# Attention and a gated feed-forward on one core: dense rows of seven tokens for the whole first batch, g's product moved, and a schedule planned with newly fitted transfers

## The chip, the cores and the metric

The kernel runs on one core of one Trainium2 chip. The metric is the device time of one execution in microseconds. Before the change three runs took 427.04, 429.23 and 430.92 us, so the median is 429.23.

## The reference

Queries and keys of 8 batches, 12 heads, 448 tokens and 64 values a head are normalized, attended, and the result goes through a feed-forward layer with a hard-swish gate.

```python
def rmsnorm(x, g):
    rms = np.sqrt(np.mean(x * x, axis=-1, keepdims=True) + 1e-06)
    return x / rms * g
q_n, k_n = (rmsnorm(q, g_q), rmsnorm(k, g_k))
scores = np.matmul(q_n, k_n.transpose(0, 1, 3, 2)) / np.sqrt(64)
attn = softmax(scores)                      # with 1e-09 added to the sum
x = np.matmul(attn, v)                      # to (3584, 768): heads side by side
h = x @ w_in                                # (768, 2048)
g = h * np.clip(h + 3.0, 0.0, 6.0) / 6.0
out = g @ w_out                             # (2048, 768)
```

All inputs and the output are float32; the matrix products run in bfloat16.

## The kernel before

Heads are taken two at a time: 8 batches of 6 pairs give 48 pairs, numbered p. The 448 tokens of a head are three tiles of 128 and a rest of 64; the rests of the two heads of a pair share one tile (number 3 in the code, NT).

*Loading* (`load_main`, `load_rest`, `load`). The queues of SyncE (SP) and ScalarE (ACT) bring q, k and v into `qk_st` and `v_st`, two pairs a transfer after the first two; GpSimd's queue (POOL) brings the weights (`next_w`, L385). For pairs below PD a head's 448 tokens lie in 64 partitions with seven consecutive tokens each, so that one transfer of 1792-byte rows brings a whole tensor (L353). Pairs below MB have the same assignment of tokens, but in the common layout of four tiles: two main transfers (L360) and one or two for the seventh token (L368, L370). Later pairs use L362 and the rest transfers.

*Statistics and normalization.* `square` (GpSimd or ScalarE, L395 and L397), `sums` (VectorE, L400), `rstd` (ScalarE, a logarithm L411 and an exponential L413), `normalize` (VectorE for pairs 0 and 1, else GpSimd; L421 for dense pairs, L423 for the others) give bfloat16 `qkn`.

*Turning.* For p below 12 TensorE transposes `qkn` (`transposes`): a dense pair takes 14 transposes of 64 by 64 for k, two of zeros, and 14 for q (L440, L443); another takes 4 of 128 by 128 each (L447). `put_k` copies k to `qkT`, `put_q` copies q and multiplies by `gprime` (L461 on VectorE). From p = 12 on a transposing transfer on SP's queue does the turning (L452). `gprime` is g_q times g_k over 8: the product is `mix_g` on VectorE (L624), TensorE turns it into a column (`turn_g`, L630), and `put_g` copies it out.

*Scores and weighing.* `score` (L470) multiplies 64 rows of k and q, the two heads of a pair side by side in the two halves of TensorE, or for the rest tile all 128 rows. ScalarE takes exponentials out of PSUM (`expo`, L486), and `weigh` (L507) multiplies by v and a column of ones, cast to bfloat16 by `cast_v` (L373). `divide` on VectorE divides by the sums; x is turned into `xT` by TensorE for p below 12 and by a transfer afterwards.

*Feed-forward.* `h_mm` (L555) forms 128 hidden columns of a batch in six products, ScalarE and VectorE apply the gate (L561, L566), `y_mm` (L574) forms 384 output columns in sixteen, ScalarE or VectorE copies them to `y_sb` (L373), and SP stores them.

*Banks.* PSUM has units 0 and 1 of two banks (`sc`), units 2, 3 and 4 of one bank (`ps`), and one bank for weighing. A step of scores of two heads takes a two-bank unit. `steps` writes scores one tile at a time for p below PB = 12, two tiles in one burst for every two pairs up to P3 = 48, and would write three from P3 on, where the first tile takes two one-bank units (`THIRD`) and `expo_head` takes its exponentials head by head. Feed-forward takes a one-bank unit or unit 1 (`FF`), and only unit 4 while a burst is due.

*The order.* It is not written by hand. `Plan` holds every operation with a rank, the engines that may run it with a price in ns, and what it depends on; it simulates the engines and transfers and issues operations in the order that results. So a constant of the plan can move any instruction of any engine. The constants for transfers say when one departs, how long it needs, and when it lands; `PRICE` and `FIRST` weigh the engines where several may do an operation.

Of the kernel before, what the change touches and what calls it, by code (L numbers as in the profile page):

```python
# [44 lines left out]
class Plan:  # L45
# [30 lines left out]
    def dma(self, key, n, size, fn, deps=(), queue="SP", hold=False, issue=None):  # L76
        op = self.add(key, [(queue, (issue or self.ISSUE) * n, fn)], deps, self.LAND, size, hold)
        op.subs, op.turn, op.ahead = n, False, 0
        return op

    def dma_transpose(self, key, size, fn, deps):
        op = self.add(key, [("SP", 1270, fn)], deps, self.LAND, size)
        op.subs, op.turn, op.ahead = 1, True, 0
        return op
# [78 lines left out]
    def begin(self, op, engine, ns, fn, now, banks):  # L163
        if banks is not None:
            op.cell["b"] = banks
            for b in banks:
                self.users[b] = list(op.parts[b] if op.parts else op.gives)
        fn()
        self.free[engine] = now + ns
        if op.subs:  # L170
            self.issued["POOL" if engine == "POOL" else "HW"] += [op] * op.subs
            self.flows[engine].append([op, op.size, now + self.DEPART])
            return
        op.end = now + ns + (op.lag or self.LAG.get(engine, 0))
        self.after(op, engine, now)

    def room(self, op, engine, now):

        old = self.issued["POOL" if engine == "POOL" else "HW"]
        n = len(old) + min(op.subs, self.DEPTH) - self.DEPTH  # L180
        return all(x.end is not None and x.end <= now for x in old[max(0, n - self.DEPTH):max(0, n)])

    def run(self):
        now = 0.0
        while self.todo or self.row or self.forced or any(self.lanes.values()):
# [6 lines left out]
            for ops in self.issued.values():  # L192
                soon += [x.end for x in ops[-3 * self.DEPTH:] if x.end is not None and x.end > now]
            best, spare = {}, None
# [53 lines left out]
def kernel(  # L248
# [33 lines left out]
    DENSE, PD, MB = 2 * NT + 1, 4, 6  # L282
# [365 lines left out]
    FF = [(4,), (3,), (2,), (1,)], [(4,)]  # L648
    THIRD = (3, 2)
# [7 lines left out]
    def x_stage(p):  # L657
        b = p // HP
        late = h_ops.get(b - NX, [])[-1:]
        if p >= XD:  # L660
            xo.append(plan.dma_transpose((p + 2, 0), 800, lambda: x_out_dma(p), [div[p]] + late))
            px.append(xo[p])
            return
        cell = {}
        xo.append(add((p + 2, 0), [("PE", 420 if p < XQ else 220, lambda: x_out(p, cell["b"][0]))], [div[p]], 165,
                      want=any_of(*ANY), cell=cell))
        px.append(add((p + 1.5, 1), [("DVE", 300, lambda: put_x(p, cell["b"][0]))], [xo[p]] + late))
        xo[p].gives = [px[p]]
# [22 lines left out]
    def h_early(f):  # L691
        cell, ops = {}, []
        for kt in range(NKT):
            ops.append(add((kt + 2, 2), [("PE", 189, lambda kt=kt: h_mm(0, f, kt, cell["b"][0]))],
                           [px[kt], at(ops, kt - 1), w_ops[piece_of(f)]] + [px[HP - 2]] * (kt == 0), 165,
                           want=any_of((2,), (3,), (4,)) if kt == 0 else None, cell=cell))
        h_ops.setdefault(0, []).append(ops[-1])
        ops[0].gives = [tail_of(0, f, len(gate_ops), ops[-1], cell)]

    def y_item(b, t, c, n, place):  # L700
# [15 lines left out]
        if (b, t) == LAST:  # L716
            ends.append(plan.dma((-1, 0), 1, 1040 * n // DM, lambda: y_store(b, t, ys, slice(c, c + n)), [out]))
        elif len(parts) == DM // YC:
            stores.append(plan.dma((-1, 0), 1 if t < NT and b * HP >= MB else 2, 1040,
                                   lambda: y_store(b, t, ys), parts))  # L720
# [18 lines left out]
    YLAG, EARLY = 0.12, 1  # L739
# [4 lines left out]
    V0, V2, LATER, AHEAD = 2.5, 0.8, -1, 3000  # L744
# [6 lines left out]
    w_ops = [plan.dma((-1, n), 1, (2600 if W_IN[n] == 256 else 4300) if n < NWI else 4700, lambda n=n: next_w(n), queue="POOL", hold=True, issue=900)  # L751
# [13 lines left out]
    def clear_slots(p):  # L765

        op = add((p - 4, 4), [("POOL", 900, lambda: clear(G, slice(p % NS, p % NS + 2))),
# [24 lines left out]
    def load(a, p, main, rest, rank, aq=nc.sync, qq="SP"):  # L792
        if main:
            op = plan.dma((p + rank, a), 2 if PD * (a < 2) <= p < MB else 1, main * 540 * (1.13 if a < 2 and p < PD else 1), lambda: load_main(aq, a, p, main), slot_free(a, p, main) + held.get(p, []), queue=qq)
# [8 lines left out]
    def load_half(a, p, rest, half, rank, aq=nc.sync, qq="SP"):  # L803
        op = plan.dma((p + rank, a + 0.1), 1, rest * (240 if a == 1 else 120),
                      lambda: load_rest(aq, a, p, rest, half), slot_free(a, p, rest) + held.get(p, []), queue=qq,
                      issue=900 if qq == "POOL" else None)
# [5 lines left out]
    def stats(p, st):  # L812
# [6 lines left out]
        if p < NFAST:  # L819
            s1 = [add((st, 2), [("POOL", 885 if p < PD else 1000, lambda a=a: square(G, p, one[a], m)),  # L820
                                ("ACT", 480 if p < PD else 530, lambda a=a: square(A_, p, one[a], m))], srcs[a] + sq_free + zeros)
                  for a in range(2)]
        else:
            s1 = [add((st, 3), [("POOL", 1640 if p < PD else 1850, lambda: square(G, p, both, m))], srcs[0] + srcs[1] + sq_free + zeros)]
        if p < 2:
# [21 lines left out]
    TS, WAIT = 12, True  # L847
    r0, AFTER_R0, AFTER_N0 = {}, {}, {1: (0,), 2: (0,)}

    def turn(p):  # L850

        old = scored.get(p - NK, [])
        if p >= TD:
            tr.append(plan.dma_transpose((p - 1, 3), 1600, lambda p=p: transposes_dma(p), norms[p] + old))
            pq.append(add((p - 1, 0), [("ACT", 560, lambda p=p: put_q(A_, p, qkT_r[p % NK][:, 1, 0:S]))], [tr[p], mg]))
            pk.append(tr[p])
        else:
            cell = {}
            if p < TS:
# [3 lines left out]
                tr.append(add((p - 0.5, 3), [("PE", 580 if p < PD else 220, lambda p=p, c=cq: transposes(p, c["b"][0], (1,)))], norms[p][1:] + old + [tk], 165,  # L863
# [8 lines left out]
            tr.append(add((p - 0.5, 3), [("PE", 1000 if p < PD else 440, lambda p=p, c=cell: transposes(p, c["b"][0]))], norms[p] + old + [idn, zero], 165,  # L872
# [9 lines left out]
    for p in range(NPAIR):  # L882
        if p == 0:
# [4 lines left out]
            lg = plan.dma((1, 1.2), 2, 40, lambda: load_g(nc.scalar), queue="ACT")  # L888
# [3 lines left out]
            load(2, 0, 2, 4, 3.5)  # L892
# [10 lines left out]
        st = p - 2 if p < HP else p + -0.5  # L903
        if p < 2:
# [19 lines left out]
        def steps(todo, pairs=None):  # L924
# [19 lines left out]
            for n, (p, i) in enumerate(todo):  # L944
# [18 lines left out]
                if last:  # L963
                    weighed[p] = w
                    div.append(add((p + 0, 0), [("DVE", 790 if p < XQ else 1170, lambda p=p: divide(p))], [w, at(xo, p - NQ), pad]))

        if p == 0:
            last_step, count, tile_of = [], {}, {}
            PB, P3 = 12, 48
# [58 lines left out]
```

## Time and profile before

| | |
|---|---|
| median of three runs | 429.23 us |
| the profiled execution | 426.02 us, span 424.2 us |
| TensorE | 408.1 us busy, 96% |
| ScalarE | 271.3 us, 64% |
| VectorE | 231.3 us, 55% |
| GpSimd | 207.0 us, 49% |
| transfers | 65.09 MB, mean 153 GB/s |

Times of instructions are durations with their pipeline. A busy TensorE counts from the start of a product to its modelled end, so products that overlap are counted once. The distance from one start to the next tells what an instruction costs its engine. In a row of the timeline, the first number is the start, the second the stretch that the row covers, xN the number of instructions in it, and in brackets the idle time before and what ended it. In a table by stretches, each engine has its busy time and its number of instructions, and the last three columns are the granted clock, the share of the transfer engines and GB/s.

### The profile page before, as it was taken

Reading aid. Unit: us, or ns where it says so; the run is one execution under the profiler, and the core shown is the slowest. Engines: PE = TensorE matmul, PEld = TensorE weight load, DVE = VectorE, ACT = ScalarE, POOL = GpSimd, SP = SyncE. Lnnn points to the kernel's source line nnn. Section 1 sums busy time; section 2 is a strip of 40 time slices with the busy share of each in tenths; the row PEclk is TensorE's granted clock in tenths of the full one; section 3 lists DMA queues with packets and bytes.
Section 4 is the critical chain, followed back from the end, with each engine's and each line's share of the span. In section 5 each row is a group of like instructions: output and inputs, shape, how many; then the busy total and the mean of one; then the engine's idle time right before and its main releaser. Section 6 shows DMA issues by size and latency. Waiting matters only on the chain.

```text
span 424.2 us, 9388 instructions
## 1 busy us (share of the span) xinstructions
PE 408.1 (96%) x3648; PEld 233.5 (55%) x3648; DVE 231.3 (55%) x470; ACT 271.3 (64%) x645; POOL 207.0 (49%) x223
## 2 busy tenths in 40 slices
PE   1979999999999999999999999999999999999996
PEld 1556655555555555555556555555556555555564
DVE  7777878556355556665655655556444443343321
ACT  4999895767867898688787878778763132132100
POOL 6889867747665567566766487767000000000000
PEclk9999999999999999999999999999999999999999
DMA  8999999996999939979798968973313200000022
GB/s 246 228 245 196 171 217 205 222 215 163 214 238 212 255 58 228 214 145 229 167 210 208 199 145 186 254 165 86 64 53 63 63 37 39 37 37 39 37 76 74
DMA packets 125663, 65.09 MB, mean 153 GB/s; under 512 B 78004, under 2 KB 122164, under 8 KB 125620
## 3 DMA queue, kind: packets, MB, share of 16 engines
q1 hardware_dynamic: 117248, 57.76, 61.3%
q0 software_dynamic: 8080, 6.29, 10.2%
q8 instruction: 28, 0.46, 0.5%
q10 hardware_dynamic: 292, 0.46, 0.3%
q14 instruction: 15, 0.12, 0.1%
HBM read 45.61 MB, written 11.01 MB: 133 GB/s over the span
## 4 chain that ended last, share of the span: by engine, by line
PE 90%; SPq 3%; DMA 3%; ACT 2%; DVE 0%; issue 0%; POOL 0%; POOLq 0%; ACTq 0%
PE ps L574 35%; PE ps L555 32%; PE av L507 10%; PE sc L470 8%; PE sc L555 2%; DMA v_st<-in_v_dram 2%; SPq L360 1%; ACT eD L486 1%; SPq L370 1%; PE ps L470 1%; DMA qk_st<-in_q_dram 1%; PE ps L447 1%; PE ps L535 0%; DVE ssq L400 0%; SPq L368 0%
## 5 line engine op out<-in xcount | busy, mean ns | idle before, releaser
L574 PE MATMUL ps<-w_out_sb,gT 128*128 128x384 bf16 (+1 forms) x912 | 170.2, 323 | 0.0
L555 PE MATMUL ps<-xT,w_in_sb 128*128 128x448 bf16 x726 | 162.2, 353 | 0.2 <-ACT eR L486 0.2
L486 ACT ACTIVATE eD<-sc 128x768 bf16<-128x768 f32 (+1 forms) x288 | 136.9, 561 | 21.4 <-PE sc L470 14.4
L561 ACT ACTIVATE t_sb<-ps 128x448 f32<-128x448 f32 x121 | 67.4, 557 | 73.9 <-PE ps L555 72.4
L574 PEld LDWEIGHTS <-gT 128*128 128x128 bf16 x912 | 82.9, 98 | 56.7 <-issue 9.6
L566 DVE SCALAR_TENSOR_TENSOR gT<-t_sb,ps 128x448 bf16<-128x448 f32 x121 | 74.5, 619 | 68.2 <-ACT t_sb L561 67.1
L423 POOL TENSOR_TENSOR qkn<-qk_st,rstd 128x512 bf16<-128x512 f32 x88 | 89.5, 1044 | 43.0 <-ACT rstd L413 42.7
L555 PEld LDWEIGHTS <-w_in_sb 128*128 128x128 bf16 x768 | 68.7, 98 | 58.4 <-issue 9.6
L397 POOL TENSOR_TENSOR sq<-qk_st 128x1024 f32<-128x1024 f32 (+2 forms) x49 | 82.3, 1691 | 7.4 <-DMA qk_st<-in_q_dram 3.7
L507 PEld LDWEIGHTS <-eD 128*128 128x128 bf16 x1152 | 53.6, 98 | 22.5 <-issue 4.9
L373 DVE COPY y_sb<-ps 128x384 f32<-128x384 f32 (+1 forms) x47 | 25.8, 549 | 69.2 <-PE ps L574 69.1
L400 DVE TENSOR_REDUCE ssq<-sq 128x16 f32<-128x1024 f32 (+2 forms) x50 | 57.6, 1160 | 7.4 <-POOL sq L397 3.5
L507 PE MATMUL av<-vaug,eD 128*128 128x65 bf16 x1152 | 60.1, 194 | 0.0
L470 PE MATMUL sc<-qkT 64*128 64x448 bf16 (+1 forms) x310 | 51.7, 361 | 3.4 <-ACT eD L486 1.8
L373 POOL CAST vaug<-v_st 128x512 bf16<-128x512 f32 x37 | 22.7, 620 | 53.2 <-PE av L507 51.7
L470 PEld LDWEIGHTS <-qkT 64*128 64x128 bf16 (+1 forms) x336 | 14.6, 94 | 28.8 <-issue 23.8
L517 DVE RECIPROCAL rden<-av 128x7 f32<-128x7 f32 x48 | 9.7, 203 | 31.9 <-PE av L507 31.6
L459 ACT ACTIVATE qkT<-qkT,gprime 128x448 bf16<-128x448 bf16 x36 | 24.5, 681 | 0.0
L523 DVE TENSOR_TENSOR xn<-av,rden 128x384 bf16<-128x384 f32 x42 | 23.4, 558 | 1.4
L507 PEld LDWEIGHTS <-eR 128*128 128x128 bf16 x240 | 16.7, 99 | 7.5 <-issue 2.3
L507 PE MATMUL av<-vaug,eR 128*128 128x130 bf16 (+1 forms) x240 | 19.4, 212 | 0.0
L486 ACT ACTIVATE eR<-sc 128x448 bf16<-128x448 f32 (+1 forms) x44 | 14.6, 387 | 7.3 <-PE sc L470 6.8
(63 smaller groups left out, 170.6 us busy)
## 6 DMA issues: line engine op xcount, KB each, us to landing
qk_st<-in_k_dram SPq DMA_DIRECT2D x21, 384.0 KB, 4.1
qk_st<-in_q_dram SPq DMA_DIRECT2D x21, 384.0 KB, 5.0
v_st<-in_v_dram SPq DMA_DIRECT2D x21, 384.0 KB, 5.9
out_dram<-y_sb SPq DMA_DIRECT2D x20, 384.0 KB, 2.3
w_out_sb<-in_moe_w_out_dram POOLq DMA_DIRECT2D x4, 768.0 KB, 10.9
out_dram<-y_sb SPq DMA_DIRECT2D x15, 192.0 KB, 3.5
w_in_sb<-in_moe_w_in_dram POOLq DMA_DIRECT2D x3, 768.0 KB, 10.2
v_st<-in_v_dram SPq DMA_DIRECT2D x22, 64.0 KB, 5.1
```

What stands on the lines that cost most here:

```text
L373: (eng.copy if eng is nc.scalar else eng.tensor_copy)(out=out, in_=in_)
L397: eng.tensor_tensor(out=sq, in0=x, in1=x, op=A_MULT)
L400: nc.vector.tensor_reduce(out=packed(p, ssq_r[:, p % NR, a]), in_=packed(p, sq_r[m % 2][:, a]), axis=mybir.AxisListType.X, op=A_ADD,)
L423: eng.tensor_tensor(out=qkn_r[p % NQ][:, a].rearrange("p t h d -> p h t d"), in0=qk_st[:, a, p % NS], in1=by[:, a].rearrange("p (h t) -> p ...
L459: eng.activation(out=out, in_=src, func=COPY, scale=gprime[:])
L470: nc.tensor.matmul(out=(bank(u[h]) if isinstance(u, tuple) else bank(u, h))[:, 0:S], lhsT=qkT[rows, 0, i * P:(i + 1) * P], rhs=qkT[rows, 1 ...
L486: nc.scalar.activation(out=out, in_=in_, func=EXP, bias=0.0, scale=1.0)
L507: nc.tensor.matmul(out=av_ps[:, c:c + n], lhsT=e_part(p, i, h, j), rhs=va[:, i].rearrange("p h d -> p (h d)")[:, h * W:h * W + n], start=f ...
L555: nc.tensor.matmul(out=bank(m)[:, 0:S], lhsT=w_in_sb[:, kt, f * P:(f + 1) * P], rhs=xT[:, kt, b % NX, x_slot(b)], start=(kt == 0), stop=(k ...
L561: nc.scalar.activation(out=t[:], in_=bank(m)[:, 0:S], func=RELU, bias=0.5, scale=1.0 / 6.0,)
L566: nc.vector.scalar_tensor_tensor(out=gT[:, f, (b % 2) * S:(b % 2 + 1) * S], in0=t[:], scalar=1.0, in1=bank(m)[:, 0:S], op0=A_MIN, op1=A_MULT,)
L574: nc.tensor.matmul(out=bank(m)[:, 0:n], lhsT=gT[:, f, c0:c0 + P], rhs=w_out_sb[:, f, c:c + n], start=(f == 0), stop=(f == NFT - 1),)
```

## The change

PD goes from 4 to 6, so k and q of pairs 4 and 5, the last two pairs of the first batch, are loaded and normalized in dense rows and turned in small pieces. `mix_g` gets the normalizations of pair 0 as predecessors, and g's two transfers rank ahead of q of pair 1. Scores go in bursts of two from pair 8 and in bursts of three from pair 24. The plan's transfers have new constants by queue, a limit of 2048 descriptors waiting in a queue, and new sizes; engines have new prices; several ranks and bank lists are changed. The core of the diff:

```diff
-    PRICE, FIRST, UNTIL = {"POOL": 0.4, "ACT": 2.0, "DVE": 1.5}, {"POOL": 0.5, "ACT": 1.7, "DVE": 1.0}, 45e3
-    ISSUE, DEPART, LAND, BULK, DEPTH = 630, 1300, 1750, 0.55, 8
-    SLOW, BEGIN, TIRED = 1.6, 3.6e3, 0.85
-    STEADY, SLACK, LATE = 70e3, 500, {"load": 3500, "turn": 2000}
+    PRICE, FIRST, UNTIL = {"POOL": 0.5, "ACT": 1.5, "DVE": 1.5}, {"POOL": 0.5, "ACT": 1.7, "DVE": 1.0}, 45e3
+    ISSUE, DEPTH, RING = 630, 8, 2048
+    DEPART, LAND, BULK = {"SP": 1330, "ACT": 1330, "POOL": 2840}, {"SP": 1200, "ACT": 1200, "POOL": 1400}, 0.64
+    SLOW, BEGIN, TIRED = 0.85, 3.6e3, 1.0
+    STEADY, SLACK, LATE = 70e3, 500, {"load": 2500, "turn": 2000}
-    DUE, SOON, FILL = 300, 0, -3000
-    LONG, LEFT = 0, 0
+    DUE, SOON, FILL = -600, 0, -3000
+    LONG, LEFT = 0.25, 0
...
+        waiting = sum(f[0].rows * f[1] / f[0].size for f in self.flows[engine])
+        if engine != "POOL" and waiting + op.rows > self.RING:
+            return False
...
-    DENSE, PD, MB = 2 * NT + 1, 4, 6
+    DENSE, PD, MB = 2 * NT + 1, 6, 6
...
-    NFAST = 10
+    NFAST = 12
-    SC, ANY = [(0,), (1,)], [(4,), (3,), (2,)]
-    RESTS = [(0,), (1,), (3,), (2,), (4,)]
+    SC, ANY = [(0,), (1,)], [(2,), (3,), (4,), (1,), (0,)]
+    RESTS = [(0,), (1,)]
-    FF = [(4,), (3,), (2,), (1,)], [(4,)]
-    THIRD = (3, 2)
+    FF = [(3,), (2,), (4,), (1,), (0,)], [(4,)]
+    THIRD = (2, 3)
...
-    YLAG, EARLY = 0.12, 1
+    YLAG, EARLY = 0.3, 1
-    V0, V2, LATER, AHEAD = 2.5, 0.8, -1, 3000
+    V0, V2, LATER, AHEAD = 2.5, 0.8, -1, 2500
...
-            lg = plan.dma((1, 1.2), 2, 40, lambda: load_g(nc.scalar), queue="ACT")
+            lg = plan.dma((0.5, 1), 2, 40, lambda: load_g(nc.scalar), queue="ACT")
+            lg.lag = 2500
-            load(2, 0, 2, 4, 3.5)
+            load(2, 0, 2, 4, V0)
...
-        st = p - 2 if p < HP else p + -0.5
+        st = p - 2 if p < HP else p + -1.5
...
-            m1 = add((-3, 0), [("DVE", 150, mix_g)], [lg, *squares[:2]])
+            m1 = add((-3, 0), [("DVE", 450, mix_g)], [lg, *norms[0]])
...
-            PB, P3 = 12, 48
+            PB, P3 = 8, 24
```

Read in order, the changed program issues v of pairs 4 and 5 on SP's queue before k and q of pairs 6 and 7 (after them in the kernel before), has g's product behind the two normalizations of pair 0 on VectorE, clears the pads of the exponentials on VectorE instead of GpSimd, and has 44 copies of y on ScalarE (10 before) and 13 on VectorE (47 before), and 19 casts of v on ScalarE (11 before).

More of the change, by code (lines that the diff above doesn't have):

```diff
@@ L193, in run @@
                 soon += [x.end for x in ops[-3 * self.DEPTH:] if x.end is not None and x.end > now]
+            if self.flows["SP"]:
+                soon.append(now + 200)
             best, spare = {}, None
@@ L793, in load @@
         if main:
-            op = plan.dma((p + rank, a), 2 if PD * (a < 2) <= p < MB else 1, main * 540 * (1.13 if a < 2 and p < PD else 1), lambda: load_main(aq, a, p, main), slot_free(a, p, main) + held.get(p, []), queue=qq)
+            op = plan.dma((p + rank, a), 2 if PD * (a < 2) <= p < MB else 1, main * (560 if a < 2 and p < PD else 920 if p < MB else 643), lambda: load_main(aq, a, p, main), slot_free(a, p, main) + held.get(p, []), queue=qq, rows=main * (128 if a < 2 and p < PD else 256))
             op.ahead = AHEAD if p >= HP else 0
@@ L847 @@
     TS, WAIT = 12, True
+    SQD, SEP = 0, 2
     r0, AFTER_R0, AFTER_N0 = {}, {}, {1: (0,), 2: (0,)}
```

51 lines of the change are left out of this document (26 added, 25 removed).

## The prediction

> **What bounds the kernel now.** I read the page, then the busy time by stretches, the timeline of the first 33 us, and the TensorE timeline of two steady places.
>
> ```profile
> span 424.2 us, 9388 instructions
> ...
> PE 408.1 (96%) x3648; PEld 233.5 (55%) x3648; DVE 231.3 (55%) x470; ACT 271.3 (64%) x645; POOL 207.0 (49%) x223
> ```
>
> ```profile
> 0.00:20.00 20.00, 10.83 (x164) 7.11 (x164) 14.71 (x43) 13.50 (x36) 15.64 (x32) 1.00 1.00 241
> 20.00:40.00 20.00, 16.99 (x251) 11.06 (x251) 14.79 (x34) 18.94 (x55) 18.10 (x22) 1.00 1.11 235
> 40.00:60.00 20.00, 20.00 (x233) 11.78 (x232) 16.04 (x37) 18.27 (x48) 14.85 (x17) 1.00 1.03 177
> ...
> 400.00:424.20 24.20, 20.67 (x143) 13.33 (x141) 5.05 (x10) 0.00 (x0) 0.00 (x0) 1.00 0.24 82
> ```
>
> ```profile
> 100.00:300.00 200.00, 199.87 (x1840) 111.08 (x1838) 112.65 (x220) 159.74 (x381) 132.16 (x129) 1.00 0.87 186
> 300.00:400.00 100.00, 99.77 (x705) 56.87 (x703) 40.97 (x81) 33.32 (x69) 1.24 (x2) 1.00 0.15 43
> ```
>
> The first columns after each stretch are its length and TensorE's busy time. TensorE is idle for 9.17 us in the first 20 us, 3.01 in the next 20, 0.13 between 100 and 300, and 3.53 in the last stretch, where the last store runs out. In between it is full. So the time is what TensorE has to do, plus the idle time of the head, plus the tail. The tail's last pieces keep their sizes and cost the same. A gain is either less TensorE work after 40 us or less idle time before. A loss is a wait in the full stretch, where nothing covers it.
>
> The profiled execution took 426.02 us, 1.8 outside its span. The median of the runs shown is 429.23, which is 0.75% more. I sum against 426.02 and carry the ratio over to the median. About 1% is what a measurement of this kernel tells from no change.
>
> **The change, part by part.** (a) *Score groups.* The planner now writes scores of pairs 8 to 11 two tiles at a time (PB 12 to 8), and of pairs 24 to 47 three at a time (P3 48 to 24).
>
> ```profile
> 210.34 0.81 PE L574 MATMUL ps<-w_out_sb,gT 128*128 128x384 bf16 x4
> 211.08 0.55 PE L470 MATMUL sc<-qkT 64*128 64x448 bf16 x4
> 211.56 1.48 PE L574 MATMUL ps<-w_out_sb,gT 128*128 128x384 bf16 x8
> 212.88 0.41 PE L507 MATMUL av<-vaug,eD 128*128 128x65 bf16 x8
> 213.13 0.49 PE L574 MATMUL ps<-w_out_sb,gT 128*128 128x384 bf16 x2
> ...
> 236.39 1.29 PE L555 MATMUL sc<-xT,w_in_sb 128*128 128x448 bf16 x6
> 237.52 1.30 PE L555 MATMUL ps<-xT,w_in_sb 128*128 128x448 bf16 x6
> ```
>
> Starts tell the cost, since durations contain the pipeline. Eight products of 384 columns take 212.88 - 211.56 = 1.32 us, so four should take 0.65; the four ahead of the scores take 0.74. Entering the half-row scores costs 0.09. Six products of 448 columns take 1.13 us, 0.19 each. The two score tiles (each a pair of half-row products side by side) should take 0.38 and take 0.48. Leaving costs 0.10. A group costs 0.19 beside its work. Before there are 3 groups for each of 12 pairs and 3 for every two of 36: 36 + 54 = 90. After, 24 + 24 + 24 = 72. Eighteen fewer, all where TensorE is full: 18 x 0.19 = -3.4 us.
>
> (b) *Dense rows of pairs 4 and 5.* Each pair is turned by 28 small transposes and 2 of zeros instead of 8 large ones.
>
> ```profile
> 18.24 0.41 PE L440 MATMUL ps<-identity,qkn 64*64 64x64 bf16 x14
> 18.48 0.20 PE L443 MATMUL ps<-identity,none 64*64 64x64 bf16 x2
> 18.61 0.36 PE L470 MATMUL sc<-qkT 64*128 64x448 bf16 x2
> ...
> 21.22 0.41 PE L440 MATMUL ps<-identity,qkn 64*64 64x64 bf16 x14
> 21.56 0.42 PE L507 MATMUL av<-vaug,eD 128*128 128x65 bf16 x8
> ...
> 25.25 0.39 PE L447 MATMUL ps<-identity,qkn 128*128 128x128 bf16 x4
> 25.48 0.41 PE L507 MATMUL av<-vaug,eD 128*128 128x65 bf16 x8
> ```
>
> From start to next start: 0.37 with the zeros, 0.34 without, against 0.23 for four large ones: 0.71 - 0.46 = 0.25 a pair, 0.5 in all. They run before 40 us, beside 3 us of idle time, so between 0 and 0.5 comes out; I take +0.3.
>
> [...]
>
> (c) *The head: g.* g's product now stands behind the two normalizations of pair 0 on VectorE.
>
> ```profile
> 4.80 1.23 DVE L400 TENSOR_REDUCE ssq<-sq 128x7 f32<-128x448 f32 x2 [0.23 <-ACT sq L395]
> 5.70 0.18 ACT L413 ACTIVATE ps<-lnv 128x7 f32<-128x7 f32 x1
> 6.30 0.18 ACT L413 ACTIVATE ps<-lnv 128x7 f32<-128x7 f32 x1
> 6.90 0.97 DVE L624 SCALAR_TENSOR_TENSOR g_two<-g_row 1x128 f32<-1x128 f32 x1 [0.87 <-DMA g_row<-in_g_k_dram]
> 7.80 1.13 DVE L421 TENSOR_TENSOR qkn<-qk_st,ps 128x448 bf16<-128x448 f32 x2
> ...
> 9.98 0.43 DVE L461 TENSOR_SCALAR qkT<-ps,gprime 128x448 bf16<-128x448 bf16 x1
> 10.46 1.02 PE L470 MATMUL sc<-qkT 128*128 128x448 bf16 x3 [0.90 <-DVE qkT L461]
> ```
>
> VectorE waits 0.87 us for g's transfer and spends 0.97 on the product, while k's factor has been there since 5.88 and q's since 6.48. Without that the normalizations start at about 6.05 and end at about 7.1 instead of 8.93. But VectorE's new order then is: product of g, copy of k, first sum of pair 1, g's column, second sum, and only then q's product (L461). By the rows: 0.97 for the product, 1.23 for the two sums, a copy like L461's 0.43, and 0.1 for the column, from 7.1 on: 9.8, or 9.5 as starts come closer than durations, against 9.98. (The copy of k was ScalarE's before; now it stands ahead.) So the first scores come 0.2 to 0.5 us earlier; pair 1's q then stands behind three short clearing writes that stood behind it. I let 0.2 survive. g's two transfers are now issued ahead of q of pair 1 on ScalarE's queue; they were in by 6.90 and are due at 7.1, and q of pair 1, two issues later, is wanted by a square behind k's. Clearing the exponentials' pads moves from GpSimd to VectorE and one pair's clearing leaves it, all ahead of 4.80, where VectorE waited 0.23; an excess over that would delay the first sum.
>
> (d) *The head: transfers.* Dense k and q of pairs 4 and 5 need 2 issues instead of 7, and v of pairs 4 and 5 is issued ahead of k and q of pairs 6 and 7.
>
> ```profile
> 16.31 1.27 SPq L360 DMA_DIRECT2D v_st<-in_v_dram  x2
> 16.71 1.00 POOL L385 DMA_DIRECT2D w_in_sb<-in_moe_w_in_dram  x1
> ...
> 26.90 0.62 POOL L373 CAST vaug<-v_st 128x512 bf16<-128x512 f32 x1 [1.21 <-DMA v_st<-in_v_dram]
> ...
> 28.07 3.03 POOL L397 TENSOR_TENSOR sq<-qk_st 128x512 f32<-128x512 f32 x3
> ...
> 29.14 1.22 DVE L400 TENSOR_REDUCE ssq<-sq 128x16 f32<-128x1024 f32 x1 [1.34 <-POOL sq L397]
> ...
> 30.39 0.21 ACT L411 ACTIVATE lnv<-ssq 128x16 f32<-128x16 f32 x1 [0.79 <-DVE ssq L400]
> ...
> 31.83 0.36 PE L470 MATMUL sc<-qkT 64*128 64x448 bf16 x2 [1.59 <-ACT eD L486]
> ```
>
> Read upwards: TensorE's longest wait after 20 us, 1.59, is for an exponential that ScalarE could not start because the statistics of pair 6 stood ahead of it. They waited for VectorE, that for GpSimd, which had waited 1.21 us to cast v of pair 4. That v was issued from 16.31 on and shared the engines with the first piece of w_in. In the new order it is ten issues further ahead (13th instead of 23rd; two take 1.27, so 6.4 us). With the same time to landing it is in near 20.4 instead of 26.8, well before 25.7, when GpSimd wants it: the 1.21 us go, and 5 us of cover are left. Next in line are k and q of pairs 6 and 7, with 16 issues ahead instead of 17, but 0.5 MB of v among them; their squares may come later, and then the same chain waits for these. I take -1.2, bounds 0 and -3.0 (all idle time of 20 to 40). With (c) the head gives -1.4, bounds 0 and -3.5.
>
> (e) *The price of bursts of three.* A burst takes four of the five score and product banks; feed-forward has one left until the first tile's two exponentials release theirs. In the trace a score pair needs 0.36 us from start to result (row at 31.83).
>
> ```profile
> L486 ACT ACTIVATE eD<-sc 128x768 bf16<-128x768 f32 x93 | 76.8, 826 | 13.1 <-PE sc L470 11.5 <-PE av L507 0.7
> L486 ACT ACTIVATE eR<-ps 128x448 bf16<-128x448 f32 x17 | 9.7, 572 | 0.2
> L373 ACT COPY y_sb<-ps 128x384 f32<-128x384 f32 x8 | 3.9, 490 | 1.5 <-PE ps L574 1.5
> L373 ACT CAST vaug<-v_st 128x512 bf16<-128x512 f32 x6 | 3.8, 634 | 0.1
> ```
>
> These are ScalarE's groups between 100 and 300 us. The split tile's first exponential is like the 572 ns row. Its bank is free at 0.1 + 0.36 + 0.57, about 1.05 us after entry; the burst is over at 3 x 0.19 + 0.19 = 0.76. So TensorE can wait 0.3 us, if the fifth bank is not yet drained and no weighing group (0.25 us, 212.88 to 213.13) is ready. If ScalarE is in the middle of an 826 ns exponential, 0.4 more. Nothing before shows such a burst; bounds are 0 and 24 x 0.7 = 16.8. Bursts of two lose only 0.13 us in 200 us, which puts it near the low end: I let one burst in three wait 0.3, +2.4 us.
>
> ScalarE also gets 9 more copies of y and 8 casts of v before its last exponential, and in each burst two of the 572 kind and a short one for one of 826 and a short one, 0.3 more: 9 x 0.49 + 8 x 0.63 + 24 x 0.3 = 17 us at most, over some 250 us, on its 80% (159.74 of 200), so 87%. What it delays is in the 0.4 above. The 25 other copies of y that leave VectorE fall behind the last exponential, where ScalarE is two thirds idle (33.32 of 100 busy).
>
> Sum: -3.4 + 0.3 - 1.4 + 2.4 = -2.1. Profiled 423.9; the ratio 0.995 of 429.23 is 427.1.
>
> **Rivals.** *Bursts starve TensorE* (slower). Place: each of the 24 bursts of the second half of the pairs. At 0.5 us each (0.3 and half of the 0.4) it costs 12.0; the sum is +7.5, the median 436.8. It turns at (3.4 + 1.4 - 0.3) / 24 = 0.19 us a burst. For it: four of five banks taken, bursts called sooner (DUE 300 to -600) with feed-forward held to one bank while one is due, ScalarE fuller. Against: 0.13 us of waits now, weighing groups to fill with. Chance 0.12.
>
> *The whole head moves up.* All 3.0 us of idle time and the 0.5 go, bursts wait for nothing: -3.4 + 0.3 - 3.5 = -6.6, the median 422.6. For it: the chain above runs through one late transfer. Against: ScalarE is 95% busy from 20 to 40. Chance 0.18.
>
> *The transfers come no earlier where it counts.* k and q of pairs 6 and 7 arrive behind v and the stall returns there: -3.4 + 0.3 + 2.4 = -0.7, the median 428.5. For it: the transfer engines' share is 1.00 and 1.11 in the first two stretches, so order alone moves no bytes. Chance 0.20.
>
> **How the numbers follow.** The forecast has 0.50, within 425.4 to 428.8. Faster by over 1% (below 424.9): the second rival and a little of the forecast, 0.20. Slower by over 1% (above 433.5): most of the first, 0.10. Within 1%: 0.70. The range 423.0 to 431.5 leaves out the larger part of the first rival and under half of the second.
>
> **What would show it.** Right: TensorE idle from 20 to 40 us about 1.6 instead of 3.0, no cast waiting 1.2 us for v; first exponential near 10.6 instead of 11.03; in a burst of three six half-row products between two starts 0.76 to 0.8 apart; idle of 100 to 300 up to some 2 us, each behind a split exponential. ScalarE's total near 300 us, VectorE's near 212 (34 copies of y and 8 casts moved). Wrong: idle above 5 us between 150 and 320 (the first rival), or idle of 3 us still in 20 to 40 (the third).

## The result and the profile after

Over 17 runs each, taken in turn, the changed kernel takes 424.88 us in the median (423.42 to 426.93) and the kernel before 427.58; the ratio is 0.9932 (95% interval 0.9914 to 0.9949), 2.7 us faster. The forecast was 0.995, within 1%; it lies just above that interval. (Its 427.1 us was reckoned from three runs of the kernel before with a median of 429.23.) The profiled execution took 423.99 us against 426.02. Its span is 422.1 against 424.2 us: -2.1, the sum of the prediction. The terms of that sum did not all come out, so each is read again.

The time of the kernel before goes with the clock that TensorE is granted: of its 68 runs in the three series of the experiments, 15 show a mean granted clock of 0.999 or 1.000 and take 425.7 us in the median, and 53 show 0.996 or less and take 427.4, while none of the changed kernel's 17 runs is below 0.999.

The page of the changed kernel, span and busy time of the engines:

```profile
span 422.1 us, 9498 instructions
...
PE 406.6 (96%) x3692; PEld 237.1 (56%) x3692; DVE 210.6 (50%) x436; ACT 291.7 (69%) x713; POOL 201.3 (48%) x215
```

The busy time by stretches of the changed kernel (length, TensorE, weight loads, VectorE, ScalarE, GpSimd, granted clock, share of the transfer engines, GB/s):

```profile
0.00:20.00 20.00, 11.25 (x184) 7.31 (x185) 15.56 (x49) 13.56 (x38) 14.33 (x28) 1.00 0.99 257
20.00:40.00 20.00, 18.59 (x280) 11.82 (x279) 12.52 (x27) 19.70 (x54) 19.44 (x26) 1.00 1.13 234
...
60.00:80.00 20.00, 19.18 (x162) 10.72 (x161) 15.79 (x29) 14.79 (x34) 14.64 (x14) 1.00 1.10 183
...
100.00:300.00 200.00, 198.75 (x1877) 114.38 (x1875) 110.29 (x221) 166.71 (x416) 126.71 (x122) 1.00 0.87 186
300.00:400.00 100.00, 99.75 (x671) 57.04 (x669) 29.96 (x57) 41.92 (x91) 0.00 (x0) 1.00 0.16 45
400.00:422.10 22.10, 19.10 (x134) 12.36 (x131) 0.00 (x0) 3.99 (x9) 0.00 (x0) 1.00 0.24 83
```

The same view of the kernel before, for the one stretch not shown yet:

```profile
60.00:80.00 20.00, 20.00 (x166) 11.43 (x165) 14.84 (x27) 13.15 (x31) 14.61 (x14) 1.00 1.26 204
```

TensorE's idle time went from 9.17 to 8.75 us in the first 20 us, from 3.01 to 1.41 in the next 20, from 0.00 to 0.82 between 60 and 80, from 0.13 to 1.25 between 100 and 300, and from 3.53 to 3.00 in the tail. In all that is -0.6. TensorE's busy time fell by 1.5, with 44 more products in it. So the time came from less work for TensorE and from the head, and the full stretch gave some of it back.

The timeline of the head, where g's product now stands behind the normalizations:

```profile
5.94 1.19 DVE L427 TENSOR_TENSOR qkn<-qk_st,ps 128x448 bf16<-128x448 f32 x2
7.05 0.27 DVE L630 SCALAR_TENSOR_TENSOR g_two<-g_row 1x128 f32<-1x128 f32 x1
...
8.91 0.44 DVE L467 TENSOR_SCALAR qkT<-ps,gprime 128x448 bf16<-128x448 bf16 x1
...
9.41 1.02 PE L476 MATMUL sc<-qkT 128*128 128x448 bf16 x3 [1.13 <-DVE qkT L467]
9.97 0.66 ACT L492 ACTIVATE eR<-sc 128x448 bf16<-128x448 f32 x2
```

The normalizations start at 5.94 instead of 7.80, and the first scores at 9.41 instead of 10.46. SyncE's queue and GpSimd's casts of v in the same kernel:

```profile
8.24 2.96 SPq L366 DMA_DIRECT2D v_st<-in_v_dram  x4
...
13.36 0.37 SPq L368 DMA_DIRECT2D qk_st<-in_k_dram  x1
```

```profile
21.99 0.61 POOL L379 CAST vaug<-v_st 128x512 bf16<-128x512 f32 x1
...
23.55 0.61 POOL L379 CAST vaug<-v_st 128x512 bf16<-128x512 f32 x1
```

The last two of the four v transfers from 8.24 on are those of pairs 4 and 5, 16.31 before. The first k of pair 6 still goes out at 13.36 (13.15 before), since the dense rows of pairs 4 and 5 took two issues in place of seven ahead of it. The casts have no wait in brackets: the 1.21 us for v are gone.

A burst of three that waits, and one that does not:

```profile
183.59 0.36 PE L476 MATMUL ps<-qkT 64*128 64x448 bf16 x2
183.65 0.53 ACT L567 ACTIVATE t_sb<-ps 128x448 f32<-128x448 f32 x1
...
183.78 0.54 PE L476 MATMUL sc<-qkT 64*128 64x448 bf16 x4
...
184.07 0.62 ACT L379 CAST vaug<-v_st 128x512 bf16<-128x512 f32 x1
...
184.58 1.04 ACT L497 ACTIVATE eD<-ps 128x448 bf16<-128x448 f32 x3
...
185.18 1.11 PE L561 MATMUL ps<-xT,w_in_sb 128*128 128x448 bf16 x5 [0.85 <-ACT eD L497]
```

```profile
199.75 0.36 PE L476 MATMUL ps<-qkT 64*128 64x448 bf16 x2
...
200.42 0.82 PE L580 MATMUL ps<-w_out_sb,gT 128*128 128x384 bf16 x4
```

In the first, ScalarE does a gate and a cast of v between the scores and the split exponentials, and feed-forward gets its bank 0.85 us late. In the second the next product starts 0.67 us after the burst did, with nothing waited for.

### The profile page after: what moved, and what is told of

Read it like the earlier page. It is cut to its first block, busy times and chain, and to the rows that moved or that the text cites. A ratio compares the mean times of both kernels' runs of the same rounds, so it can differ in the third digit from the quotient of the medians.

```text
span 422.1 us, 9498 instructions
## 1 busy us (share of the span) xinstructions
PE 406.6 (96%) x3692; PEld 237.1 (56%) x3692; DVE 210.6 (50%) x436; ACT 291.7 (69%) x713; POOL 201.3 (48%) x215
## 4 chain that ended last, share of the span: by engine, by line
PE 81%; ACT 5%; DMA 5%; issue 2%; DVE 2%; POOL 2%; SPq 1%; POOLq 0%; DVEq 0%; ACTq 0%
PE ps L580 34%; PE ps L561 29%; PE av L513 9%; PE sc L476 6%; DMA v_st<-in_v_dram 3%; ACT eD L492 3%; DMA qkT<-qkn 2%; PE ps L476 1%; DMA qk_st<-in_q_dram 1%; POOL qkn L429 1%; DVE ssq L406 1%; ACT t_sb L567 1%; PE ps L446 1%; SPq L376 1%; PE sc L561 1%
## 5 line engine op out<-in xcount | busy, mean ns | idle before, releaser
L561 PE MATMUL ps<-xT,w_in_sb 128*128 128x448 bf16 x750 | 165.4, 352 | 1.5 <-ACT eD L497 1.1
L580 PE MATMUL ps<-w_out_sb,gT 128*128 128x384 bf16 (+1 forms) x896 | 162.5, 323 | 0.0
L572 DVE SCALAR_TENSOR_TENSOR gT<-t_sb,ps 128x448 bf16<-128x448 f32 x125 | 76.9, 620 | 110.5 <-ACT t_sb L567 109.6
L492 ACT ACTIVATE eD<-sc 128x768 bf16<-128x768 f32 x240 | 113.3, 567 | 6.0 <-PE sc L476 5.6
L429 POOL TENSOR_TENSOR qkn<-qk_st,rstd 128x512 bf16<-128x512 f32 x84 | 85.2, 1043 | 25.0 <-ACT rstd L419 24.7
L567 ACT ACTIVATE t_sb<-ps 128x448 f32<-128x448 f32 x125 | 69.8, 562 | 31.1 <-PE ps L561 28.5
L379 ACT COPY y_sb<-ps 128x384 f32<-128x384 f32 (+1 forms) x43 | 20.6, 478 | 57.4 <-PE ps L580 57.3
L379 POOL CAST vaug<-v_st 128x512 bf16<-128x512 f32 x29 | 17.7, 620 | 39.2 <-PE av L513 38.7
L497 ACT ACTIVATE eD<-ps 128x448 bf16<-128x448 f32 (+2 forms) x72 | 25.1, 419 | 15.7 <-PE ps L476 15.7
L492 ACT ACTIVATE eR<-sc 128x448 bf16<-128x448 f32 x96 | 32.9, 412 | 3.1 <-PE sc L476 2.9
```

Source lines behind the costliest of these rows:

```text
L379: (eng.copy if eng is nc.scalar else eng.tensor_copy)(out=out, in_=in_)
L429: eng.tensor_tensor(out=qkn_r[p % NQ][:, a].rearrange("p t h d -> p h t d"), in0=qk_st[:, a, p % NS], in1=by[:, a].rearrange("p (h t) -> p ...
L492: nc.scalar.activation(out=out, in_=in_, func=EXP, bias=0.0, scale=1.0)
L497: nc.scalar.activation(out=e[:, c:c + cols.stop - cols.start], in_=src[:, cols], func=EXP, bias=0.0, scale=1.0)
L561: nc.tensor.matmul(out=bank(m)[:, 0:S], lhsT=w_in_sb[:, kt, f * P:(f + 1) * P], rhs=xT[:, kt, b % NX, x_slot(b)], start=(kt == 0), stop=(k ...
L567: nc.scalar.activation(out=t[:], in_=bank(m)[:, 0:S], func=RELU, bias=0.5, scale=1.0 / 6.0,)
```

## The experiments

Kernels named f_ keep the planned order of all instructions as it was, written out as a list (`script`), and move only what the diff names. Those named u_ (from the changed kernel) and d_ (from the kernel before) change a constant and are planned anew, so that everything behind it can move too. Ratios are to the kernel before, run in turn in the same series.

**Is a score group worth 0.19 us?** The third tile of each of the 24 bursts goes behind the next piece of TensorE's work.

```diff
+        for first in triples:
+            third = first.chain[-1]
+            x = script.pop(where(third))
...                                          # i: the next operation on TensorE behind the burst
+            script.insert(i + 1, x)
```

> The changed kernel with every order kept except that in each of the 24 bursts of three the third tile's scores are issued on TensorE behind the next operation, so that every burst is two groups. Theory (a group of half-row scores costs TensorE 0.19 us for entering and leaving): 24 x 0.19 = 4.6 us more, ratio near 1.004. Rival (the switch is hidden by the products that run on, and only the waits for banks count): under 1 us more.

Measured: 1.0063 (1.0038 to 1.0087), 429.62 us; span 427.8. The page:

```profile
PE 411.8 (96%) x3692; PEld 237.2 (55%) x3692; DVE 210.8 (49%) x436; ACT 292.7 (68%) x713; POOL 201.1 (47%) x215
```

TensorE does the same 3692 products and is busy 5.2 us longer: entry and exit of a group count as busy. The span is 5.7 longer, 0.24 us a group; 0.93 of it is more idle time between 60 and 80 us, which differs from run to run (0.8 to 1.9 in all kernels with the new order), and without that it is 0.20. The first theory holds, and the rival is out.

**Do bursts of three pay, waits included?**

```diff
-            PB, P3 = 8, 24
+            PB, P3 = 8, 48
```

> The changed kernel with no bursts of three: pairs 24 to 47 in bursts of two as before (P3 = 48), planned anew. Theory (steps a and e): 12 more groups cost 12 x 0.19 = 2.3 us and the waits of about 2.1 us behind the bursts of three go; 0.2 us slower than the changed kernel, ratio to before 0.994. Rival 1: the waits are not the bursts' own and stay; 2.3 us slower, 0.998. Rival 2: bursts of three cost more than their waits show; 1.5 us faster, 0.990.

Measured: 0.9946 (0.9917 to 0.9974), 425.08 us. The stretches:

```profile
100.00:300.00 200.00, 200.00 (x1831) 110.69 (x1830) 108.73 (x214) 167.19 (x395) 128.82 (x124) 1.00 0.91 187
300.00:400.00 100.00, 100.00 (x716) 57.09 (x714) 32.52 (x65) 41.65 (x86) 1.24 (x2) 1.00 0.15 44
```

All waits between 100 and 400 us are gone, and TensorE is busy 2.3 us longer (408.9 against 406.6), the price of 12 more groups. The waits are the bursts' own: they take 1.5 of those 2.3 us. The span is 1.0 us longer (423.1), and the time is that of the changed kernel within the intervals, so that what bursts of three still gain is less than the runs can tell.

**g's product alone, from both sides.** In f_g the changed kernel has it ahead of the normalizations again, with g's transfers behind q of pair 1. In f_bg the kernel before gets the new place and the earlier transfers.

```diff
+        x = script.pop(where(m1))                                        # f_g
+        script.insert(min(where(n) for n in norms[0]), x)
+        x = script.pop(where(lg))
+        script.insert(where(landed[1][1][0]) + 1, x)
...
+        x, y, z = (script.pop(where(o)) for o in (m1, m2, mg))           # f_bg
+        script.insert(max(where(n) for n in norms[0]) + 1, x)
+        i = where(tr[0]) + 1
+        script[i:i] = [y, z]
+        x = script.pop(where(lg))
+        script.insert(where(landed[1][1][0]), x)
```

> The changed kernel with every engine's order kept except for g: its product stands on VectorE ahead of the two normalizations of pair 0 again, and g's two transfers behind q of pair 1 on ScalarE's queue. Theory (the earlier first scores reach the feed-forward stream): the first score comes back from 9.4 to about 10.4 us and the median rises by 0.6 to 1.0 us over the changed kernel, so the ratio to the kernel before is near 0.995. Rival (ScalarE is full from 20 to 40 us and absorbs it): the first score is as late, and the median stays within 0.2 us of the changed kernel's (0.993).

> The kernel before with every order kept except for g: product behind the normalizations of pair 0, its turn on TensorE behind the transposes of pair 0, its transfers ahead of q of pair 1. Theory (the stall for v behind it eats the gain): the first score comes 0.5 to 1.0 us earlier than 10.46, the idle time of TensorE between 20 and 40 us grows by as much, and the median stays within 0.3 us of the kernel before (ratio 0.999 to 1.001). Rival (a microsecond gained at the start is a microsecond at the end): ratio near 0.998.

Measured: f_g 0.9958 (0.9934 to 0.9983), f_bg 1.0037 (1.0020 to 1.0055). The first scores of f_g start at 9.95, 0.54 later than in the changed kernel:

```profile
9.95 1.02 PE L482 MATMUL sc<-qkT 128*128 128x448 bf16 x3 [1.13 <-DVE qkT L473]
```

Its span is 1.0 longer, again with 1.0 more idle time between 60 and 80, so that g is worth between nothing and 1.1 us there (0.9958 - 0.9932 = 0.26%), and the run can't tell more. On the kernel before the ratio fits neither theory: the move is a loss. The stall that the first one named is there (idle time of TensorE from 20 to 40 us goes from 3.01 to 4.20), and of the gain nothing is left even in the first 20 us (9.22 idle against 9.17). GpSimd and TensorE in f_bg:

```profile
28.72 0.62 POOL L379 CAST vaug<-v_st 128x512 bf16<-128x512 f32 x1 [2.80 <-DMA v_st<-in_v_dram]
```

```profile
33.65 0.36 PE L476 MATMUL sc<-qkT 64*128 64x448 bf16 x2 [3.26 <-ACT eD L492]
```

First scores were a microsecond earlier (9.45 against 10.46), and the head ran into the late v harder: 2.80 us of wait in place of 1.21, and 3.26 on TensorE in place of 1.59. The clock is lower, too: 8 of the 12 runs of f_bg show a mean granted clock of 0.992 or less, 3 of 18 of the kernel before.

**v's place in the queue alone, from both sides.** In f_v v of pairs 4 and 5 goes behind k and q of pairs 6 and 7 in the changed kernel, in f_bv ahead of them in the kernel before, and f_bvg adds g's move to f_bv.

```diff
+        vs = [script[where(o)] for o in landed[2][4]]
+        script[:] = [s for s in script if s not in vs]
+        at_ = max(where(o) for a in (0, 1) for o in landed[a][6]) + 1      # f_v; f_bv: min(...)
+        script[at_:at_] = vs
```

> The changed kernel with every order kept except on SP's queue, where v of pairs 4 and 5 goes behind k and q of pairs 6 and 7 again. Theory (the late v was the stall of 20 to 40 us): GpSimd's cast of pair 4 waits for v again, idle time of TensorE between 20 and 40 us goes from 1.4 back to about 3, and the median rises by 1.2 to 1.6 us (ratio near 0.997). Rival (the dense rows make the transfers early enough in any order): no wait for v, the idle time stays under 2 us, the median within 0.4 us.

> The kernel before, its planned order kept, with the six transfers of v of pairs 4 and 5 moved ahead of the five of k and q of pairs 6 and 7 on SyncE's queue, and nothing else. Theory (step d of the prediction): v is in before GpSimd wants it, the wait of 1.21 us for it goes, TensorE's idle time from 20 to 40 us falls from 3.0 to about 1.8; ratio to before 0.997. Rival (transfers come no earlier where it counts): k and q of pairs 6 and 7 are five or six issues later, 3 to 4 us, their squares are late instead, idle time stays at 3 us or grows; ratio 1.000 to 1.005.

> The kernel before, its order kept, with both moves: v of pairs 4 and 5 ahead of k and q of pairs 6 and 7, and g's product behind pair 0's normalizations with g's transfers ahead of q of pair 1. Theory: the move of g alone cost 0.4% because the head that it brought forward ran into the late v (a wait of 2.80 us, 3.3 us of TensorE's idle time, and a granted clock of 0.5 for 3.3 us after it); with v ahead it keeps about 1 us, and the two together give 0.995. Rival: g's move harms by itself (its transfers delay q of pair 1 or v), and the ratio is 1.000 or more whatever v does.

Measured: f_v 1.0109 (1.0087 to 1.0131), 431.43 us. Far above both theories. Its timelines of GpSimd and TensorE and one stretch:

```profile
27.09 0.62 POOL L385 CAST vaug<-v_st 128x512 bf16<-128x512 f32 x1 [5.14 <-DMA v_st<-in_v_dram]
```

```profile
31.20 0.58 PE L452 MATMUL ps<-identity,qkn 64*64 64x64 bf16 x14 [5.39 <-POOL qkn L433]
...
41.81 0.36 PE L567 MATMUL ps<-xT,w_in_sb 128*128 128x448 bf16 x1
```

```profile
32.00:34.00 2.00, 2.00 (x27) 1.39 (x25) 0.78 (x3) 0.98 (x4) 1.98 (x5) 0.50 0.25 56
```

The planned order has GpSimd cast v of pair 4 where it thought v had landed. The cast waits 5.14 us, the normalizations of pair 5 stand behind it, and TensorE stands still for 5.39 us. Then it works at a granted clock of 0.50.

f_bv measured 1.0020 (1.0000 to 1.0040), f_bvg 1.0007 (0.9986 to 1.0027). The rival of f_bv holds. In f_bvg the rival's ratio came out, but not its reason: with v ahead, g's move does not harm (1.0007 beside 1.0020, within the intervals), and GpSimd waits for k of pair 6 in both, 4.22 us in f_bvg. GpSimd and TensorE in f_bv:

```profile
25.76 1.04 POOL L403 TENSOR_TENSOR sq<-qk_st 128x512 f32<-128x512 f32 x1 [3.51 <-DMA qk_st<-in_k_dram]
```

```profile
27.86 0.61 PE L453 MATMUL ps<-identity,qkn 128*128 128x128 bf16 x4 [3.25 <-POOL qkn L429]
```

v is in time, and k of pair 6 is late in its stead: GpSimd waits 3.51 us for it. This is the third rival of the prediction, seen where the order alone moves.

**Which part of that loss is the order on GpSimd?** f_vp is f_v with both casts of v behind pair 5's normalizations.

```diff
+        for n in (5, 4):
+            x = script.pop(where(vc[n]))
+            script.insert(max(where(n) for n in norms[5]) + 1, x)
```

> The changed kernel with v of pairs 4 and 5 behind k and q of pairs 6 and 7, as in the run that took 1.0109, and now GpSimd's two casts of v of pairs 4 and 5 are behind pair 5's normalizations too; nothing else. Theory: the loss came from GpSimd's fixed order, since the cast that waited 5.14 us for v held the normalizations of pair 5, and the 5.4 us in which TensorE then stood still lowered its granted clock to 0.5 for 6.7 us. With the casts behind, TensorE stands still for under 2 us at a time, the granted clock stays at 1.00, and the ratio to before is 0.995 to 0.998. Rival: the bytes are late whatever the order; TensorE waits for the weighing of pair 4 or for pair 6 instead, idle time from 20 to 40 us stays near 5 us, ratio 1.008 or more.

Measured: 1.0032 (1.0011 to 1.0054), between the two. Moving the casts wins back 0.77% of the 1.77% that lie between f_v and the changed kernel. In the timelines the wait has shrunk and moved on:

```profile
30.46 1.18 POOL L385 CAST vaug<-v_st 128x512 bf16<-128x512 f32 x2 [2.92 <-DMA v_st<-in_v_dram]
```

```profile
34.63 0.56 PE L459 MATMUL ps<-identity,qkn 128*128 128x128 bf16 x4 [3.72 <-POOL qkn L435]
```

Now pair 6's normalizations stand behind the casts. TensorE still stands still for 3.72 us, and the granted clock falls to 0.50 from 34.7 to 38.1 us, where the first theory expected 1.00. Both theories had a part: a strict order on GpSimd, and bytes that are late whatever the order.

**What does the halved clock cost?** f_vfill is f_v with 26 unread products in the place where TensorE stood still.

```diff
+        for _ in range(26) if p == 5 and 0 in which else ():
+            nc.tensor.matmul(out=bank(b)[:, 0:S], lhsT=identity[:], rhs=qkT_r[(p - 1) % NK][:, 0, 0:S], ...)
```

> The changed kernel with v of pairs 4 and 5 behind k and q of pairs 6 and 7 (the run at 1.0109), and 26 products of 448 columns that nobody reads ahead of pair 5's transposes of k, in the place where TensorE stood still for 5.4 us; they add 26 x 0.187 = 4.9 us of work inside the wait. Theory: the clock itself cost time. Kept busy, TensorE keeps a granted clock of 1.00, the 4.1 us of work that it did at 0.5 after the wait take 2.05, and the kernel is 2 us faster than that run, ratio to before 1.006. Rival: the half clock cost nothing since other engines set the pace after the wait; ratio 1.010 to 1.012 whatever the clock shows.

Measured: 1.0121 (1.0078 to 1.0163), as slow as f_v. Its timeline and one stretch:

```profile
25.61 5.09 PE L449 MATMUL ps<-qkT,identity 128*128 128x448 bf16 x26
31.55 0.41 PE L454 MATMUL ps<-identity,qkn 64*64 64x64 bf16 x14 [0.85 <-POOL qkn L433]
...
41.41 0.36 PE L569 MATMUL ps<-xT,w_in_sb 128*128 128x448 bf16 x1
```

```profile
32.00:34.00 2.00, 2.00 (x37) 1.36 (x37) 1.36 (x4) 1.36 (x5) 2.00 (x4) 1.00 0.31 68
```

In this execution the clock stays at 1.00. From pair 5's transposes to the first feed-forward product it takes 41.41 - 31.55 = 9.86 us, against 41.81 - 31.20 = 10.61 in f_v. So the half clock cost 0.75 us there, not 2. That is 0.18% of the run, less than the intervals can tell. The rival's ratio holds; that behind the wait the other engines set the pace fits, and is argued. Most of the loss is standing still: f_v's span is 7.3 us longer than the changed kernel's, and TensorE is idle for 4.4 us more between 20 and 40 us and for some 2 us more elsewhere.

**The dense rows and the fitted transfers, planned anew.**

```diff
-    DENSE, PD, MB = 2 * NT + 1, 4, 6
+    DENSE, PD, MB = 2 * NT + 1, 6, 6      # d_dense, in the kernel before; u_dense: back to 4
...
+    ISSUE, DEPTH, RING = 630, 8, 10 ** 9  # u_fit: DEPART, LAND, BULK, SLOW, TIRED, LATE, AHEAD
+    ...                                   # and the sizes of transfers as before
```

> The kernel before with k and q of pairs 4 and 5 in dense rows too (PD = 6), planned anew with the old transfer model; no bursts, no new order of g. Theory: dense rows take 2 issues in place of 7, 3 us of SyncE's queue, so that v of pairs 4 and 5 and k and q of pairs 6 and 7 can both come in time, which the move of v alone could not do (there k of pair 6 was late by 3.51 us); idle time from 20 to 40 us falls by about 1.2, transposes add 0.5; ratio to before 0.997 to 0.999. Rival: the rows help only together with an order planned for them; without the new transfer model a wait over 2 us is left and the ratio is 1.002 or more.

> The changed kernel with k and q of pairs 4 and 5 in seven issues as before (PD = 4), planned anew with the new transfer model. Theory: SyncE's queue is 3 us longer ahead of v of pairs 4 and 5 and of k and q of pairs 6 and 7, one of them is late, TensorE stands still for over 3 us and its granted clock falls to 0.5 for some 3 to 7 us; 4 to 6 us slower than the changed kernel, ratio to before 1.002 to 1.007. Rival (dense rows are only a cost of 0.5 us): ratio 0.992.

> The changed kernel planned with the transfer model of before (its latencies, rates, sizes and due times put back); dense rows, bursts and g as changed. Theory: the order of the first 30 us is what the fit decides; with the old model v or k and q are late again and TensorE stands still for over 2 us from 20 to 40 us; 3 us or more above the changed kernel, ratio to before 1.000 or more. Rival: dense rows and bursts carry the gain and the fit is worth under 1 us; ratio 0.993 to 0.995.

Measured: d_dense 1.0059 (1.0029 to 1.0088), u_dense 1.0238 (1.0188 to 1.0287), u_fit 1.0121 (1.0083 to 1.0158). The rows alone do not help without an order for them: the rival of d_dense holds. In its profiled execution, one of the longest of its 12 runs (432.79 us, median 429.67), TensorE waits early for an exponential, and at 36.8 us the granted clock drops. The drop is not the whole loss: the five runs with a mean clock of 1.000 take 428.3 to 429.7 us, while the kernel before takes 425.6 to 426.2 in those at 0.999 or more:

```profile
18.03 0.56 PE L470 MATMUL sc<-qkT 64*128 64x448 bf16 x2 [2.31 <-ACT eD L486]
```

```profile
33.40:36.80 3.40, 2.05 (x38) 1.41 (x36) 1.94 (x4) 3.33 (x11) 3.40 (x4) 1.00 1.26 232
36.80:43.80 7.00, 6.40 (x55) 3.93 (x56) 4.12 (x10) 5.09 (x14) 6.96 (x9) 0.51 0.86 165
```

u_dense and u_fit are slower, as the first theory of each said. u_dense has the idle time that it named (3.47 us from 20 to 40), but loses more elsewhere, and u_fit does not have it. The stretches of u_dense, then of u_fit:

```profile
20.00:40.00 20.00, 16.53 (x247) 10.96 (x246) 15.13 (x30) 19.84 (x56) 19.77 (x25) 1.00 0.99 239
...
100.00:300.00 200.00, 193.97 (x1780) 110.29 (x1778) 108.08 (x210) 160.23 (x398) 127.67 (x123) 1.00 0.91 190
```

```profile
20.00:40.00 20.00, 19.21 (x299) 12.35 (x297) 14.52 (x33) 19.19 (x52) 16.41 (x23) 1.00 1.06 229
...
100.00:300.00 200.00, 196.04 (x1764) 111.15 (x1763) 103.10 (x202) 158.42 (x390) 108.80 (x102) 1.00 0.83 170
300.00:400.00 100.00, 99.60 (x751) 56.49 (x748) 39.15 (x78) 54.18 (x126) 16.69 (x14) 1.00 0.30 76
```

u_fit has less idle time from 20 to 40 us than the changed kernel (0.79), but 3.96 between 100 and 300, and GpSimd does 16.69 us of its work after 300 where the changed kernel does none: attention has fallen behind. In u_dense 6.03 us are idle from 100 to 300, where its theory had nothing: another plan. So these three show that the plan depends on each constant, not what one constant is worth by itself.

## Why the prediction was right, step by step

(a) *Score groups: the price right, the count a little high.* 0.19 us (u_burst) to 0.24 measured against 0.19. In the traces 87 groups became 71, since some that the count of 90 and 72 holds apart stand side by side: sixteen fewer, 3.0 us at 0.19. TensorE's busy time fell by 1.5 only. If the dense rows cost 0.5, as forecast, some 1 us of that difference has no term.

(b) *Dense rows: not measured alone.* Both kernels with another PD were planned anew, and the term of 0.3 us can't be read out of them.

(c) *g: the term was mis-sized.* With the change as a whole, first scores came 1.05 us earlier (10.46 to 9.41), not 0.2 to 0.5. The step took 0.97 us for the product, from the row of before. With its data there, it takes 0.27 (0.28 in f_g), so 0.7 of the 0.97 was not the product. Of what came earlier 0.42 us were left in the first 20 us. And "that g's move can be priced by itself" was a silent assumption: on the kernel before it costs 0.37%, where the stall that it runs into was still there.

(d) *Transfers: the size about right, the reason half of it.* Idle time of 20 to 40 us went from 3.01 to 1.41 (forecast about 1.6), and no cast waits for v. With (c) the head gave 2.0 us against 1.4. But the step counted "ten issues further ahead" for v and one fewer for k and q as two facts. They are one: v goes ahead without making k late because five issues of dense rows left the queue. Moved alone, v's place brings the third rival's stall (3.51 us on k of pair 6) and a ratio of 1.002.

(e) *Bursts: half the sum, and another kind.* Idle time between 100 and 400 us grew by 1.1 us. All of TensorE's waits for split exponentials are these two, 1.1 us in all (view of L497):

```profile
who waited for it (us, times):
  PE ps L561: 1.1, 2
```

From start to next start, 22 of the 24 bursts take 0.67 or 0.68 us, as 200.42 - 199.75 shows, one takes 1.59 (at 183.59) and one 0.99 (at 310.53): 1.2 us lost, against 2.4. Not one burst in three waits 0.3: most wait for nothing, and one waits nearly a microsecond when ScalarE has taken something else in between. The first rival, 12 us of starving, is out. (The "four of the five banks" of the prediction are four of five units, six of seven banks.)

*Not foreseen.* Between 60 and 80 us 0.82 us of idle time are new. The timeline:

```profile
78.19 0.67 ACT L465 ACTIVATE qkT<-qkT,gprime 128x448 bf16<-128x448 bf16 x1 [1.47 <-DMA qkT<-qkn]
...
78.91 0.35 PE L476 MATMUL sc<-qkT 128*128 128x448 bf16 x1 [0.82 <-ACT qkT L465]
```

A transposing transfer for the third batch (pairs from 12 on) is late there; the prediction looked at the transfers of the head alone. The tail gave 0.5 us back.

*Luck in the sum.* As far as the terms can be measured, groups gave 3.0 us instead of 3.4, the head 2.0 instead of 1.4, and the bursts cost 1.1 instead of 2.4. Outside the sum, the 0.8 at 60 to 80 us and the 1 us without a term are lost, and 0.5 is won in the tail. That all this comes to -2.1 again is luck. The direction is not, nor are the places: fewer groups, the late v, waits behind split exponentials.

*A term that is not in the sum: the clock.* The sum compares two executions at a granted clock of 1.00 and carries the ratio over to the median, but most runs of the kernel before are not at 1.00. f_g and u_burst, both close to the changed kernel, are 2.3 and 2.1 us under the kernel before in their series, but only 1.1 and 0.6 us under those of its runs that show 0.999 or more (4 and 7 runs). So about half of the measured gain or more goes with a drop of the clock that the kernel before mostly has and the new order mostly has not. How much of that is the clock's own cost, and how much the longer wait that comes with it, stays open.

*By its own signs:* first exponential at 9.97 (forecast near 10.6), 0.67 us from a burst to the next product (0.76 to 0.8), ScalarE 291.7 and VectorE 210.6 us (near 300 and 212), the idle time of 100 to 300 at 1.25 with the largest wait behind a split exponential.

*Still open:* which work is the 1 us without a term; what the dense rows are worth alone; why u_fit's TensorE is busy 4.8 us longer than the changed kernel's with as many products; which part of the new order brought the late transfer at 78 us.

## What to carry to other kernels

An early part made faster met the next late transfer sooner here (in f_bg first scores came 1.01 us earlier, and the wait for v grew from 1.21 to 2.80): price such edits together with the queue they run into, since three of them, each made without the others, lost 0.2 to 0.6% and the whole won 0.7%. An operation placed where the plan thought its data would be can hold what stands behind it on its engine: in f_v one cast waited 5.14 us for late data, and TensorE stood still for 5.39. A large group of products saved its entry and exit here (0.19 to 0.24 us), and paid for it in banks (0.85 us of wait at the worst); look for what the engine that frees the banks does between. One profiled execution can be a rare one (that of the kernel before is at 1.00, and 53 of its 68 runs in the experiments at 0.996 or less): compare its granted clock with that of the runs before a sum is carried over to the median.

## What the runs showed of the hardware

In these runs the granted clock halved after stretches in which TensorE did little, and not only when it did nothing. In f_v it is 0.50 from 28.6 to 35.4 us, after 25.8 to 28.6 without a product; in f_bg 0.53 on average from 34.8 to 38.4, after 3.4 us with 1.15 of work; in d_dense 0.51 over 7.0 us, after 3.4 us with 2.05 of work (rows above), and in f_bv likewise:

```profile
22.60:26.00 3.40, 2.00 (x27) 1.22 (x25) 1.57 (x4) 3.32 (x9) 0.24 (x1) 1.00 1.12 252
26.00:33.00 7.00, 5.14 (x49) 3.26 (x49) 3.14 (x6) 3.31 (x9) 6.95 (x9) 0.51 1.07 221
```

By stretches of 0.2 to 0.4 us the low clock lasted 3.4 us in f_bg and f_vp and 6.8 us in f_v, d_dense and f_bv. The runs give no limit for the work in the stretch before: in the profiled execution of the kernel before, the 3.4 us from 28.6 hold 1.75 us of work, less than in d_dense and f_bv, and the clock stays at 1.00, while 53 of its 68 runs in the three series show a mean clock of 0.996 or less.

At the start TensorE is slow for longer than the clock column shows. In the changed kernel 14 transposes take

```profile
15.87 0.58 PE L446 MATMUL ps<-identity,qkn 64*64 64x64 bf16 x14
...
17.32 0.41 PE L446 MATMUL ps<-identity,qkn 64*64 64x64 bf16 x14
```

0.58 us at 15.87 and 0.41 at 17.32, while the clock column says 1.00 all along (this trace holds no clock record before 16.35 us). All groups of 14 from the first at 6.61 to the one at 15.87 take 0.58, the pace of f_v's row at 31.20 (0.58 too), where the granted clock is 0.50. In u_fit that pace lasts longer: in its chain of work (`--critical`) two score products take 0.49 us at 19.61 and three transposes of x 0.43 at 20.09, against 0.29 at 42.38 and 0.34 at 41.55. Work moved into the first 16 us is dearer here than its price later, 0.58 us against 0.41 for 14 transposes.
